# Another start address for the output weights of the second MoE in each half stretch of blocks

## The chip, the cores and the metric

The kernel runs on one core of a Trainium2 chip. Its time is the device time of one execution in microseconds (us), and the number that counts is the median of several executions. Five engines work side by side and meet at semaphores: TensorE (PE, with its weight loads shown apart as PEld), VectorE (DVE), ScalarE (ACT), GpSimd (POOL) and SyncE (SP). DMAs are issued from the queues of SP, ACT and POOL and carried out by 16 DMA engines.

## What is computed

A chunked attention, then two feed-forward blocks ("MoE" in the names), all in float32 from input to output:

```
attention:  out[c] = softmax(q[c] k_full.T / 8) v_full     # 24 chunks of 32 rows, 8 heads, batch 4
first MoE:  xn = x / rms(x) * rms_g                        # 3072 tokens, 512 columns
            y  = (silu(xn @ w_gate) * (xn @ w_val)) @ w_out    # 1536 inner columns
second MoE: h  = y @ w_in                                  # 2048 inner columns
            g  = h if h >= 1, 0 if h <= -1, else (h + 1)^2 / 4
            out = g @ w_out                                # [2048, 512]
```

The change touches the operand of the last line alone: the second `w_out`.

## The kernel before

**Stages.** Six token tiles of 512 tokens go through the kernel. The first four are done one at a time by the plain first MoE, with the attention of later tiles in the gaps. The last two go through the first MoE as a pair, in a form with 7 products in place of 8 (`proj1`, then `out1p`). Then the second MoE takes the six tiles as three pairs: `proj2` makes the inner columns, `out2` multiplies them by `w_out`.

**Precision by three products.** Each float32 operand is kept as a high and a low part (type fp32r), and each product is three matmuls: high times high, high times low, low times high. A matmul has a stationary operand (128 columns, loaded by a weight load) and a moving operand (512 columns, streamed past it).

**`out2`.** It writes tokens on the rows, so the inner columns `hi`, `lo` are stationary and the weights move. For one block b (128 inner columns) and each of 4 token groups m it runs L990 to L992: `hi` against `wh`, `hi` against `wl`, `lo` against `wh`. So a block is 12 matmuls, all of which read one weight tile `wo` of 128 x 2 x 512 (high part, then low part; 4096 bytes in each partition). There are 16 blocks in each of the six calls (3 pairs, and o = 0 or 1 in each pair), 96 blocks in all, 1152 matmuls.

**Order of the work.** In a pair, each `proj2(g)` of g = 0 to 7 is 42 matmuls, and behind it stand two blocks of `out2` with o = 0 (from g = 1 on; in the later pairs, g = 0 is followed by the last two blocks of the pair before). After the eighth come the last two blocks of o = 0 and 14 blocks of o = 1 in a row; the last two of o = 1 wait for the next pair, or end the kernel.

**The weight ring.** `load_wo(i)` takes a tile from a pool with four buffers under the tag `wo` and has SP load it from the DRAM tile `w2o_d` (pieces of 2048 bytes). Blocks 4 to 95 are loaded behind the last matmul of the block four earlier (`load_wo(i + 4)`). The first MoE uses the same function and the same tag for its own 24 loads (i below `2 * F1` = 24), with the weights as stationary operand (L546 to L548). Its call for i = 24 to 27 already draws four tiles of the second MoE from the first MoE's pool `p1`; these are loaded and not read, and the same four blocks are loaded again from the pool `m2` when the second MoE begins. So there are 100 loads from `w2o_d`.

**Queues near the first pair.** SP carries out its DMAs in the order of the program. At the start of the pair of the first MoE it issues four `wo` loads and behind them the loads of `wall` from `w1p_d` (`load_wp`, L763), on which `proj1` runs. POOL's queue at that time still writes converted weights of the second MoE to DRAM (`lo_s`, L200 and L201, from the tile `s12` or `s34`). A tile that is placed where an earlier one lay waits for the last reader of the earlier one, DMAs included.

Of the kernel before, what the change touches and what calls it, by code (L numbers as in the profile page):

```python
# [9 lines left out]
F32R = mybir.dt.float32r  # L10
# [6 lines left out]
P = 128  # L17
# [13 lines left out]

TT = 512
PT = 256
D = 64
FILL = 352

# [2 lines left out]
def tile_stream_attention_moe_moe2(  # L39
# [12 lines left out]
    F1 = wts1.shape[0] // 3  # L52
    F2 = wts2.shape[0] // 2
    KK = DM // P
    NTT = NT // TT
    NU = q.shape[0]
    SCALE = 1.0 / float(D) ** 0.5

    pool = lambda name, bufs, **kw: ctx.enter_context(tc.tile_pool(name=name, bufs=bufs, **kw))
# [245 lines left out]
    m2 = {"single": True, "pace": 0.0}  # L305
# [43 lines left out]
    def load_qk(u):  # L349
# [5 lines left out]
        else:  # L355
            kt = [att.tile([P, TT], F32, tag=f"k{hp}", name="k_in") for hp in range(2)]
            qt = att.tile([P, 2 * PT], F32, tag="q", name="q_in")
        for hp in range(2):
# [4 lines left out]
    def load_v(u):  # L363
        if u >= NU:
            return
        n = 8 * (D + 1)
        if u < 4:
            if not tails:
                tails.append(xs.tile([P, 4, 2, D + 1], F32, tag="xn", name="v_tail"))
            tail = tails[0][:, u]  # L370
            nc.sync.dma_start(tail, v[u].rearrange("p (h c) -> p h c", h=2)[:, :, n - D - 1:])
            vt = [xs.tile([P, TT], F32, tag=f"x{'hl'[hp]}{u}", name="v_in") for hp in range(2)]
            m = n - D - 1
        else:
# [9 lines left out]
    def step_s(u, ps):  # L384
        kt, qt = qk_t.pop(u)
        for hp in range(2):
            for blk in range(2):
                for j in range(4):
                    for par in range(2):
# [4 lines left out]
                            ps[32 * j:32 * j + 32, par, o:o + 64],  # L394
                            qt[p0:p0 + 64, hp * PT + 32 * c:hp * PT + 32 * c + 32],
                            kt[hp][p0:p0 + 64, 64 * c:64 * c + 64],
# [51 lines left out]
    def part_n(u):  # L448
        pr, hh = divmod(u, 2)
        ps = ps_t.pop(("v", u))  # L450
        if hh == 0:
# [8 lines left out]
        nc.vector.tensor_scalar(  # L460
            out=rd.unsqueeze(3), in0=ov[:, :, :, D:D + 1], scalar1=1e-9, scalar2=None, op0=ALU.add
        )
# [144 lines left out]
    for st in ORDER.split():  # L607
        c, n = st[0], st[1:]
# [32 lines left out]
        elif c in "HL":  # L641
            kk, o = divmod(n, 2)
            part = slice(o * PT, o * PT + PT)
            if c == "H":
# [3 lines left out]
        elif c == "G":  # L648
            cols = slice(n % 2 * PT, n % 2 * PT + PT)
            for x in x_t[n // 2]:  # L650
# [101 lines left out]
    wo = {}  # L752
# [12 lines left out]
    def load_wo(i):  # L765

        if i < 2 * F1:
            src = w1o_d[i % F1]
        elif i < 2 * F1 + 2 * NP2 * F2:
            n, u = divmod((i - 2 * F1) % F2, 2)  # L770
            src = w2o_d[n][:, :, u]
        else:
            return
        if i in (0, 2 * F1):
            m2["limit"] = 2 * F1 if i == 0 else 1 << 30
        if i < m2["limit"]:
            wo[i] = m2["pool"].tile([P, 2, 512], F32R, tag="wo", name="wo", bufs=4)
            nc.sync.dma_start(wo[i].bitcast(F32), src)


# [186 lines left out]
    def out1p(o, blocks):  # L967

        last = F1 - 1 in blocks and len(blocks) > 1
        order = [(f, m) for m in range(KK) for f in blocks] if last else [(f, m) for f in blocks for m in range(KK)]  # L970
        for f, m in order:
            sl = slice(m * P, (m + 1) * P)
            w = wo[o * F1 + f]
            mm3(ps_y[m], (w[:, 0, sl], w[:, 1, sl]), hs["1", f, o], f == 0, f == F1 - 1)
            if m == KK - 1:
                load_wo(o * F1 + f + 4)
            if f == F1 - 1:
                evac(m, y_d[NS + o][:, m], nc.sync)

    def out2(pr, o, blocks):  # L980

        M = range(TT // P)
        last = F2 - 1 in blocks
        order = [(b, m) for m in M for b in blocks] if last else [(b, m) for b in blocks for m in M]
        for b, m in order:
            sl = slice(m * P, (m + 1) * P)
            i = 2 * F1 + (2 * pr + o) * F2 + b
            hi, lo = hs[F2 * pr + b, o]
            wh, wl = wo[i][:, 0], wo[i][:, 1]
            nc.tensor.matmul(ps_y[m], hi[:, sl], wh, start=b == 0, stop=False)  # L990
            nc.tensor.matmul(ps_y[m], hi[:, sl], wl, start=False, stop=False)  # L991
            nc.tensor.matmul(ps_y[m], lo[:, sl], wh, start=False, stop=b == F2 - 1)  # L992
            if m == TT // P - 1:
                load_wo(i + 4)
            if b == F2 - 1:
                evac(m, rows(2 * pr + o, m), nc.scalar)
# [17 lines left out]
    for i in range(4):  # L1014
        load_wo(i)
# [45 lines left out]
def _layouts(i):  # L1061
# [4 lines left out]
    M = i["mem_k"].shape[2]  # L1066
    C, NP = S // _CHUNK, S // PT
    W = _CHUNK + _LEFT + _RIGHT + M

    def heads(a):  # L1070

        return a.reshape(B, H // 4, 2, 2, NP, C // NP, *a.shape[3:])
# [20 lines left out]
    q = heads(i["q"].reshape(B, H, C, _CHUNK, D))  # L1093
    q = q.transpose(0, 4, 1, 3, 7, 2, 5, 6).reshape(B * NP * H // 4, 2 * D, 2 * PT)
    kw = heads(kw).transpose(0, 4, 1, 3, 7, 2, 5, 6).reshape(B * NP * H // 4, 2 * D, -1)
# [44 lines left out]
```

## Time and profile before

| | |
|---|---|
| median of 3 runs | 1179.24 us (1176.91 to 1180.4) |
| span of the profiled execution, first to last instruction | 1172.9 us |
| PE busy | 1151.0 us, 98% of the span |
| DVE, ACT, POOL busy | 741.2, 517.6, 108.0 us |
| mean DMA rate | 238 GB/s |
| chain of work that ended last | 86% PE, 6% DMA, 4% DVE |

The span leaves out what lies before the first and after the last instruction: 1179.24 - 1172.9 = 6.3 us against the median. "Busy" counts each matmul from its start to its modelled end; matmuls overlap in the pipeline, so what a matmul costs is the time from its start to the start of the next one, and not its duration.

### The profile page before, as it was taken

The numbers are of one execution on the slowest core, as the hardware profiler recorded it, in microseconds if no ns is written. First come the engines' busy times: TensorE is split into PE (matmuls) and PEld (weight loads), VectorE is DVE, ScalarE is ACT, GpSimd is POOL, SyncE is SP. The second block draws the span as 40 slices with busy tenths as digits, with TensorE's granted clock in tenths as the row PEclk, the third lists the DMA queues.
The fourth block names the chain that finished last, engine by engine and source line by source line (L and its number), as shares of the span: only waits on it lengthen the run. The fifth ranks groups of instructions, "written<-read, shape, count | busy, mean of one in ns | idle before, by whom it ended". The sixth has DMA issues, their size and how long they took to land.

```text
span 1172.9 us, 19949 instructions
## 1 busy us (share of the span) xinstructions
PE 1151.0 (98%) x7993; PEld 936.4 (80%) x7993; DVE 741.2 (63%) x1280; ACT 517.6 (44%) x910; POOL 108.0 (9%) x175
## 2 busy tenths in 40 slices
PE   6899999999999999999999999999999999999998
PEld 4677878887778778878888888888888888888887
DVE  5888865566465655877677576665376662576620
ACT  4766756556665664433333343333143341343310
POOL 2200012212122122201111000000000000000000
PEclk9899999999999999999999999999999999999999
DMA  8566467788767666598898775757466576555364
GB/s 307 177 221 208 153 223 275 282 290 294 276 206 239 223 199 225 199 383 311 305 361 309 283 279 189 261 187 267 158 222 260 195 259 203 191 190 197 135 202 157
DMA packets 98589, 278.60 MB, mean 238 GB/s; under 512 B 10560, under 2 KB 22848, under 8 KB 92096
## 3 DMA queue, kind: packets, MB, share of 16 engines
q1 hardware_dynamic: 79936, 218.59, 52.5%
q0 software_dynamic: 15104, 52.44, 12.3%
q10 hardware_dynamic: 3456, 6.29, 1.4%
q8 instruction: 63, 1.03, 0.3%
q14 instruction: 30, 0.25, 0.1%
HBM read 209.13 MB, written 68.16 MB: 236 GB/s over the span
## 4 chain that ended last, share of the span: by engine, by line
PE 86%; DMA 6%; DVE 4%; ACT 2%; issue 1%; POOL 0%; SPq 0%; ACTq 0%; DVEq 0%; POOLq 0%
PE ps_y L991 7%; PE ps_y L992 7%; PE ps_y L990 7%; PE ps_g L546 6%; PE ps_g L547 6%; PE ps_g L548 6%; PE ps_b L855 5%; PE ps_b L854 5%; PE ps_b L856 5%; PE ps_y L546 5%; PE ps_y L547 5%; PE ps_y L548 5%; PE ps_g L854 4%; PE ps_g L855 4%; PE ps_g L856 4%; DMA w<-in_w_dram 3%
## 5 line engine op out<-in xcount | busy, mean ns | idle before, releaser
L546 PE MATMUL ps_g<-xh,wall 128*128 128x512 f32 x384 | 156.3, 407 | 0.0
L547 PE MATMUL ps_g<-xl,wall 128*128 128x512 f32 x384 | 150.9, 393 | 0.0
L548 PE MATMUL ps_g<-xh,wall 128*128 128x512 f32 x384 | 150.4, 392 | 0.0
L914 ACT ACTIVATE t<-t,half 128x512 f32<-128x512 f32 x96 | 69.0, 720 | 131.2 <-DVE t L913 131.2
L991 PE MATMUL ps_y<-wo,wall 128*128 128x512 f32 x324 | 126.0, 389 | 0.0
L990 PE MATMUL ps_y<-wo,wall 128*128 128x512 f32 x324 | 126.0, 389 | 0.0
L992 PE MATMUL ps_y<-wo,wall 128*128 128x512 f32 x324 | 126.0, 389 | 0.0
L854 PE MATMUL ps_b<-wall 128*128 128x512 f32 x288 | 112.0, 389 | 0.0
L855 PE MATMUL ps_b<-wall 128*128 128x512 f32 x288 | 112.0, 389 | 0.0
L856 PE MATMUL ps_b<-wall 128*128 128x512 f32 x288 | 112.0, 389 | 0.0
L928 DVE TENSOR_TENSOR t<-t,ps_g 128x512 f32<-128x512 f32 x24 | 16.5, 688 | 113.5 <-PE ps_g L856 107.9
L548 PEld LDWEIGHTS ps_g<-xh,wall 128*128 128x128 f32 x384 | 72.6, 189 | 16.1
L854 PE MATMUL ps_g<-wall 128*128 128x512 f32 x216 | 84.2, 390 | 1.1 <-DMA wall<-w1p_d 1.0
L546 PEld LDWEIGHTS ps_g<-xh,wall 128*128 128x128 f32 x384 | 72.6, 189 | 15.8
L855 PE MATMUL ps_g<-wall 128*128 128x512 f32 x216 | 84.1, 389 | 0.0
L856 PE MATMUL ps_g<-wall 128*128 128x512 f32 x216 | 84.0, 389 | 0.0
L547 PEld LDWEIGHTS ps_g<-xl,wall 128*128 128x128 f32 x384 | 72.8, 190 | 13.5
L546 PE MATMUL ps_y<-hh,wall 128*128 128x512 f32 x192 | 77.6, 404 | 0.0
L547 PE MATMUL ps_y<-hl,wall 128*128 128x512 f32 x192 | 75.2, 392 | 0.1
L548 PE MATMUL ps_y<-hh,wall 128*128 128x512 f32 x192 | 74.9, 390 | 0.0
L990 PEld LDWEIGHTS ps_y<-wo,wall 128*128 128x128 f32 x324 | 60.8, 188 | 12.7
L991 PEld LDWEIGHTS ps_y<-wo,wall 128*128 128x128 f32 x324 | 60.8, 188 | 12.6
(157 smaller groups left out, 2240.4 us busy)
## 6 DMA issues: line engine op xcount, KB each, us to landing
wo<-w2o_d SPq DMA_DIRECT2D x100, 512.0 KB, 4.8
wall<-w2p_d SPq DMA_DIRECT2D x24, 1792.0 KB, 7.3
wall<-w1p_d SPq DMA_DIRECT2D x12, 1792.0 KB, 8.6
w<-in_w_dram SPq DMA_DIRECT2D x36, 512.0 KB, 3.9
w<-in_w_dram POOLq DMA_DIRECT2D x32, 512.0 KB, 5.5
k_in<-in_k_dram SPq DMA_DIRECT2D x48, 256.0 KB, 4.6
wo<-w1o_d SPq DMA_DIRECT2D x24, 512.0 KB, 7.9
v_in<-in_v_dram SPq DMA_DIRECT2D x40, 260.0 KB, 4.3
```

Source lines behind the costliest of these rows:

```text
L546: nc.tensor.matmul(ps, wh, xh, start=start, stop=False)
L547: nc.tensor.matmul(ps, wh, xl, start=False, stop=False)
L548: nc.tensor.matmul(ps, wl, xh, start=False, stop=stop)
L854: nc.tensor.matmul(bank, wh, xh, start=st, stop=False, skip_group_check=True)
L855: nc.tensor.matmul(bank, wh, xl, start=False, stop=False, skip_group_check=True)
L856: nc.tensor.matmul(bank, wl, xh, start=False, stop=kk == 1, skip_group_check=True)
L914: nc.scalar.activation(s, s, AF.Square, scale=0.5, bias=half)
L928: tt(out=u2, in0=a, in1=b2, op=ALU.add)
L990: nc.tensor.matmul(ps_y[m], hi[:, sl], wh, start=b == 0, stop=False)
L991: nc.tensor.matmul(ps_y[m], hi[:, sl], wl, start=False, stop=False)
L992: nc.tensor.matmul(ps_y[m], lo[:, sl], wh, start=False, stop=b == F2 - 1)
```

## The change

The tile drawn for a block of the second MoE gets 1152 columns in place of 1024 (4608 bytes in each partition in place of 4096), and the weights lie in it from column `STARTS[k]` on, where k counts half stretches of eight blocks (two to each of the six calls of `out2`). `F2` is 16, so k runs from 0 to 11. The twelve offsets are 8, 16, 24, 48, 4, 56, 64, 96, 128, 192, 256 and 384 bytes.

```diff
+STARTS = (2, 4, 6, 12, 1, 14, 16, 24, 32, 48, 64, 96)
...
         if i < m2["limit"]:
-            wo[i] = m2["pool"].tile([P, 2, 512], F32R, tag="wo", name="wo", bufs=4)
+            if i < 2 * F1:
+                wo[i] = m2["pool"].tile([P, 2, 512], F32R, tag="wo", name="wo", bufs=4)
+            else:
+                k = (i - 2 * F1) // (F2 // 2)
+                w = m2["pool"].tile([P, 1152], F32R, tag="wo", name="wo", bufs=4)
+                wo[i] = w[:, STARTS[k]:STARTS[k] + 1024].rearrange("p (h c) -> p h c", h=2)
             nc.sync.dma_start(wo[i].bitcast(F32), src)
```

No engine gets another instruction or another order. What else moves is addresses. In the built programs every buffer of `wo` in `m2` begins 32 bytes past a multiple of 64, before and after (4608 is 72 times 64), so before the change all 96 blocks are read from such a start, and after it from 40, 48, 56, 16, 36, 24, 32, 0, 32, 32, 32 and 32 bytes past a multiple of 64, for k = 0 to 11. The tiles `h0` to `h4` and `e2` behind the ring move up by 2048 bytes. Since the tag `wo` of pool `p1` also gets the larger size, three of the four buffers of the first MoE's own loads move up by 1536, 1024 and 512 bytes; the one that moves by 1536 now also covers part of the old tile `s34`.

That changes some waits. On SP, at the start of the first MoE's pair, this stood before (names in brackets are the semaphores that the DMA waits for; DMASW are those of DMAs from POOL's queue, DMAHW those from the other queues):

```order
L778 DMA wo<-w1o_d_144 128x1024 [waits PE_49]
L778 DMA wo<-w1o_d_145 128x1024 [waits DMASW7_49,DMASW3_49]
L778 DMA wo<-w1o_d_146 128x1024 [waits DMASW7_49]
L778 DMA wo<-w1o_d_147 128x1024 [waits DMAHW3_49]
L763 DMA wall<-w1p_d_134 128x3584 [waits DMASW2_49,DMAHW4_49,DMASW1_49,DMAHW5_49,DMASW0_49,PE_49]
```

and this stands there now:

```order
L784 DMA wo<-w1o_d_144 128x1024 [waits PE_49]
L784 DMA wo<-w1o_d_145 128x1024 [waits DMASW5_49,DMASW7_49,DMASW3_49,DMASW1_49]
L784 DMA wo<-w1o_d_146 128x1024 [waits DMASW7_49]
L784 DMA wo<-w1o_d_147 128x1024 [waits DMAHW3_49]
L764 DMA wall<-w1p_d_134 128x3584 [waits DMAHW4_49,DMASW2_49,DMAHW5_49,DMASW0_49,PE_49]
```

The second of the four loads has taken over the wait for DMASW1 (the DMA out of `s34`), which before stood at no `wo` load, and one for DMASW5.

## Rows read from the trace of the kernel before

**Rows 1.** The page: busy time by engine, granted clock in 40 slices.

```profile
PE 1151.0 (98%) x7993; PEld 936.4 (80%) x7993; DVE 741.2 (63%) x1280; ACT 517.6 (44%) x910; POOL 108.0 (9%) x175
PEclk9899999999999999999999999999999999999999
```

**Rows 2.** PE's waits: line, releaser, us in total, times, longest.

```profile
PE ps_a L519 <- ACT xn L535: 2.7, 1, 2.7
...
PE ps_g L854 <- DMA wall<-w1p_d: 1.0, 1, 1.0
```

**Rows 3.** Timeline of PE in `out2`: start us, us, what; 12 starts apart.

```profile
1125.42 0.39 PE L991 MATMUL ps_y<-wo,wall 128*128 128x512 f32 x1
...
1128.14 0.39 PE L991 MATMUL ps_y<-wo,wall 128*128 128x512 f32 x1
```

**Rows 4.** Timeline of PE in `proj1`, where `wall` moves; 12 starts apart.

```profile
619.91 0.39 PE L856 MATMUL ps_g<-wall 128*128 128x512 f32 x1
...
622.63 0.39 PE L856 MATMUL ps_b<-wall 128*128 128x512 f32 x1
```

**Rows 5.** Stretches: us, busy (count) by engine, granted clock, DMA share, GB/s.

```profile
8.00:20.00 12.00, 6.68 (x310) 5.05 (x298) 5.80 (x13) 3.62 (x7) 0.00 (x0) 0.97 1.05 375
...
497.00:508.00 11.00, 11.00 (x50) 9.13 (x49) 7.87 (x13) 4.40 (x8) 1.43 (x3) 1.00 1.00 390
508.00:520.00 12.00, 11.09 (x49) 8.83 (x48) 10.55 (x18) 5.39 (x9) 1.24 (x2) 1.00 1.03 425
...
720.00:745.00 25.00, 25.00 (x112) 20.71 (x111) 17.04 (x29) 9.51 (x15) 0.00 (x0) 1.00 0.67 243
...
798.96:820.72 21.76, 21.76 (x97) 18.02 (x96) 13.63 (x12) 7.09 (x7) 0.00 (x0) 1.00 0.71 241
...
1125.39:1147.15 21.76, 21.76 (x97) 18.02 (x96) 0.69 (x1) 0.00 (x0) 0.00 (x0) 1.00 0.72 240
```

**Rows 6.** Timeline of PE: fill matmuls, transposes, attention with 64 and 65 columns.

```profile
8.62 0.77 PE L95 MATMUL ps_s<-busy 128*128 128x352 bf16 x4
...
159.20 0.60 PE L423 MATMUL ps_a<-ident,e 128*128 128x128 f32 x4
162.47 0.86 PE L393 MATMUL ps_a<-k_in,q_in 64*32 64x64 f32 x64
166.25 0.86 PE L439 MATMUL ps_a<-v_in,aT 64*32 64x65 f32 x64
```

**Rows 7.** Lines L423 and L95 on PE: count, duration ns min/median/max, first and last.

```profile
L423 PE MATMUL ps_a<-ident,e x76: 270/272/327, 65.9 to 429.4; 128*128 128x128 f32 x76
...
L95 PE MATMUL ps_s<-busy x16: 312/322/501, 8.6 to 37.5; 128*128 128x352 bf16 x16
```

**Rows 8.** Issues of `wo` in 1128:1150 us: duration, then issue to landing.

```profile
L778 SPq DMA_DIRECT2D wo<-w2o_d x9: 517/517/519, 1128.1 to 1149.9; - x9
...
DMA to landing us min/median/max: 3.3/4.3/5.3
```

**Rows 9.** The page, DMA issues: count, KB each, median us to landing.

```profile
wo<-w2o_d SPq DMA_DIRECT2D x100, 512.0 KB, 4.8
...
v_in<-in_v_dram SPq DMA_DIRECT2D x8, 227.5 KB, 4.8
v_tail<-in_v_dram SPq DMA_DIRECT2D x4, 65.0 KB, 5.2
```

**Rows 10.** Timeline of POOL near 496 us.

```profile
495.50 0.65 POOL L201 DMA_DIRECT2D w2p_d<-s  x1 [1.32 <-DVE s L199]
...
496.69 0.54 POOL L201 DMA_DIRECT2D w2p_d<-s  x1
```

**Rows 11.** Timeline of SP's queue near 500 us.

```profile
499.56 6.09 SPq L778 DMA_DIRECT2D wo<-w1o_d  x4
506.88 0.32 SPq L763 DMA_DIRECT2D wall<-w1p_d  x1
```

**Rows 12.** Line L201 in 494:499 us: time to landing of its two DMAs.

```profile
DMA to landing us min/median/max: 8.4/9.6/10.8
```

**Rows 13.** SP's waits: line, releaser, us in total, times, longest.

```profile
SPq L778 <- DMA w2p_d<-s: 2.1, 1, 2.1
```

**Rows 14.** Timeline of PE where `proj1` first waits for `wall`.

```profile
518.70 0.39 PE L548 MATMUL ps_y<-wall,wo 128*128 128x512 f32 x1
520.06 0.47 PE L854 MATMUL ps_g<-wall 128*128 128x512 f32 x1 [0.97 <-DMA wall<-w1p_d]
```

**Rows 15.** The chain that ended last, that place: start us, us, what.

```profile
506.88 13.04 DMA wall<-w1p_d
```

## The prediction

> **What bounds the kernel now.** I read the page first: PE is busy 98% of the span, and its clock stands at the upper of its two levels (2.4 GHz) in nearly every slice [rows 1]. A busy share of matmuls can hide gaps, so the list of PE's waits comes next: the longest is 2.7 us, and from the first MoE's pair to the end only one wait for a DMA is left, 0.97 us for `wall` [rows 2, 14]. So whatever lengthens a matmul's turn on PE lengthens the kernel by the same amount, and whatever the DMAs or SP do costs nothing until it passes its slack. The changed operand is the moving one of `out2`, so I then took the distance of starts there. In [rows 3] twelve starts take 1128.14 - 1125.42 = 2.72 us, 226.7 ns each, and the window of a half stretch holds 96 turns (and one cut by its edge) in 21.76 us [rows 5]: 96 x 226.7 ns = 21.76 us, nothing idle. The durations of 0.39 us in these rows are longer than a turn, since matmuls overlap. Where `wall` moves in place of `wo`, twelve starts take 622.63 - 619.91 = 2.72 us too [rows 4].
>
> The sum is made on the profiled execution, 1172.9 us of span; 6.3 us lie around it against the median of 1179.24, and I carry them over unchanged. A difference of 0.3% is 3.5 us, about what a measurement can tell from none. Half stretches pass that only together or at a high price: 3.5 us over 96 turns is 37 ns a matmul in one of them, or 3 ns in all twelve.
>
> **The change, part by part.**
>
> *Instructions and order.* None added, none removed, the same order on each engine: 0 us.
>
> *PE's reads of `wo`.* The 1152 matmuls of `out2` read 512 columns (2048 bytes in each partition) from a new start. The trace shows no fp32r matmul from such a start, since every moving tile of that type begins 32 bytes past a multiple of 64. The cost is bounded from both sides. Above: the four transposes of [rows 6] move float32 columns at (0.60 - 0.27)/3 = 109 ns for 128 columns (0.27 is the median duration [rows 7]), so 436 ns for 512: a read that fell to that rate would cost 209 ns a turn, 20.1 us in a half stretch. Below: the four fill matmuls (bf16, 352 columns) take (0.77 - 0.32)/3 = 150 ns a turn (0.32 from [rows 7]), so 218 ns for 512: 8.6 ns less a turn, 0.83 us in a half stretch, 9.9 us in all twelve. I take 0. The nearest rows are the two attention rows of [rows 6]: one reads 64 columns from starts 256 bytes apart, the other 65 columns from starts 260 bytes apart, so three of four of its starts are off a multiple of 16 bytes and half are off a multiple of 8. Both take 0.86 us for 64 instructions. They are plain float32 and so short that their issue may set the pace, which keeps a cost of less than a factor possible; that is why both ends stay in the range.
>
> The Trainium skill, "SBUF — State Buffer" (Door 1, the box on cachelines) says that memory lines are 16 bytes long and that each step to a new line pays a penalty. By it a start off a multiple of 16 (k = 0, 2, 4, 5) touches 129 lines in place of 128; an estimate from that page is under 1% of a turn, some 0.7 us over those four half stretches, and the time by it 1180.4 us in place of 1179.7. The same page says under "Operand start alignment" that any multiple of the element size is legal and that its runs timed nothing; no run here shows more yet.
>
> *Weight loads.* `h0` to `h4` move by 2048 bytes and keep their place within 64 bytes, and so do the first MoE's `wo` tiles (512, 1024, 1536 bytes): 0 us.
>
> *DMAs into `wo`.* Same number, size and pieces. In the 14 blocks in a row each load is issued behind block b for block b + 4, whose turn comes three blocks later: 3 x 2.72 = 8.16 us. Landing takes 3.3 to 5.3 us there [rows 8], so about 2.9 us are free. DMAs are busy 0.71 to 0.72 of that time at 240 GB/s [rows 5], of which `wo` moves 524 kB per 2.72 us = 193 GB/s, so about 0.58 of the share. It takes pieces 1.5 times as long before 0.72 + 0.29 reaches 1 and the ring runs dry. The one transfer in the trace that already lands at starts off 16 bytes is `v_tail` (65 columns a piece): 5.2 us to landing against 4.8 us for its neighbour `v_in` [rows 9]. That is 0.4 us, hidden in 2.9 us: 0 us.
>
> *The new wait on SP.* The second `wo` load of the first MoE's pair now waits until the DMA out of `s34` has landed. POOL issues its two DMAs from L201 at 495.50 and 496.69 us [rows 10]; they take 8.4 and 10.8 us [rows 12], so they land at 503.9 and 507.5. SP today waits 2.1 us for the first of them at the third load [rows 13], and gets to the load of `wall` at 506.88, when PE has freed its buffer [rows 11]. Now SP stands still until about 507.5, and behind it are queued three `wo` loads and that load of `wall`, for which PE waits already. With 0.32 us [rows 11] to 0.9 us for each of the three loads before it, `wall` is issued at about 508.6 to 510.2: 1.7 to 3.3 us later. That would be PE's loss if its 13.04 us to landing [rows 15] were latency. They are mostly queue: DMAs are busy 1.00 of the time from 497 to 520 us, at 390 to 425 GB/s [rows 5], so a later issue delays little as long as transfers that are queued already fill the engines. Ends: 0 and 3.3 us; I take 0.5 us, nearer the lower end by those shares. Loads behind wait for PE and not for SP: no more.
>
> *Waits in the second MoE.* The first use of `h1` to `h3` now names other DMAs, loads into `p1` from the end of the first MoE, while those tiles are first written behind several products; the first load into `m2` loses one wait: 0 us.
>
> Sum: 0 + 0 + 0 + 0 + 0.5 + 0 = +0.5 us: 1172.9 to 1173.4 of span, 1179.7 us of time.
>
> **The rivals.**
>
> *An odd start halves the read (slower).* If PE takes fp32r columns in pairs or lines, a start off that unit could cost a second access for each. It decides from 37 ns a turn in one half stretch. Its price at the rate of the transposes is 20.1 us: with the 4-byte offset alone (k = 4) 1199.8 us, with all four starts off 16 bytes (k = 0, 2, 4, 5) 1179.7 + 80.4 = 1260.1. A smaller toll, 10 ns a turn in the six half stretches that start off 32 bytes, is 5.8 us: 1185.5. Against it stand the two equal attention rows, for it that they may be paced by their issue.
>
> *A better start is faster.* A turn of 226.7 ns is 8.6 ns above the rate of the fill matmuls. If the start 32 bytes past a multiple of 64 were the reason, k = 7 alone would be cured (it starts at a multiple of 64): 0.8 us, not to be told from nothing. Only if most other starts cure it too does it count: all but the five that keep the 32 (k = 6, 8 to 11), so seven half stretches, give 5.8 us: 1173.9. For it: all streams share that start and that rate. Against: nothing but bf16 shows another rate.
>
> The Trainium skill, "TensorE: Matmul & The Clock Gate" (Back-to-back issue gap), gives 216 ns for an isolated turn of 512 columns at the upper clock; this trace shows 226.7, and no run here says yet what the 11 ns are; were all of them due to the start and cured in those seven half stretches, the time by that page would be 1172.3 us.
>
> *DMAs into odd starts are slow (slower).* If pieces landing off a multiple of 32 bytes (k = 0 to 5) took twice as long, the share in the 14 blocks in a row (k = 2 and 3) would go to 0.72 + 0.58 = 1.30, and PE would wait 0.30 x 21.76 = 6.5 us in each: 13 us, 1192.7. Between `proj2` the share is 0.67 at 243 GB/s [rows 5] and `wo` is two loads in 42 + 24 turns (14.96 us, 70 GB/s) there, so 0.19 of it: 0.86, no wait. It decides from 1.5 times. Against it: `v_tail`.
>
> *The wait on SP costs its whole bound.* 3.3 us: 1182.5, which is still within 0.3%; only with a second miss of `wall` behind it is it more.
>
> **How the numbers follow.** No change that counts (1176.2 to 1182.8): 0.74, by the equal rates of all streams and the hidden DMAs. Odd start: 0.13, of which 0.06 small and 0.07 at 1199 and over. Slow DMAs 0.04, more from SP's wait 0.03: slower 0.20. Faster by a better start: 0.06. The range runs from 1176 to 1188, which takes in the forecast with the upper end of SP's wait and the small toll (0.74 + 0.06 + 0.03 = 0.83) and leaves out the gain and the high prices.
>
> **What would show it.** Right: starts in `out2` 226.7 ns apart in all twelve half stretches, windows of 21.76 us, no wait of PE for `wo`; SP's four loads ending near 508 and PE's wait for `wall` near 520 us between 1 and 4 us. Wrong: a half stretch with another distance of starts (the odd start if it is k = 4, or 0, 2, 4, 5; the better start if shorter); or PE waiting for `wo` with a landing over 8 us in k = 2, 3 (slow DMAs).

## The result and the profile after

| | before | after |
|---|---|---|
| median of 4 runs each | 1179.80 us (1176.91 to 1180.4) | 1185.18 us (1184.7 to 1186.66) |
| ratio after / before | | 1.0058 [1.0036, 1.008] |
| span of the profiled execution | 1172.9 us | 1182.9 us |
| PE busy | 1151.0 us | 1156.8 us |

By the ratio of the runs the change made the kernel slower by 0.36 to 0.8%, more than the 0.3% that a measurement can tell from nothing; the two medians alone are 5.4 us apart, 0.46%. The time lies in the predicted range; the case held for the likeliest, no change, did not come. The profiled execution after took 1184.7 us, 1.8 us more than its span. So of the 6.3 us between the span of before and its median, about 1.8 lie around the span, and the rest is that this execution lay below the median (1172.9 + 1.8 = 1174.7 us, less than each of the four runs). The span difference of 10.0 us therefore holds some run-to-run variation, and the ratio is the better measure.

First one line of `out2` from the page of before, then the engines and the lines of `out2` from the page of after (columns of the lines: line, engine, names and shapes, count, busy us, mean ns of one, idle before). L996 to L998 are L990 to L992 of before; L860 of `proj1` is for comparison. The last line is the DMA issue that answers to [rows 9].

```profile
L991 PE MATMUL ps_y<-wo,wall 128*128 128x512 f32 x324 | 126.0, 389 | 0.0
```

```profile
PE 1156.8 (98%) x7993; PEld 936.0 (79%) x7993; DVE 740.2 (63%) x1280; ACT 517.2 (44%) x910; POOL 107.6 (9%) x175
...
L996 PE MATMUL ps_y<-wo,wall 128*128 128x512 f32 x324 | 127.9, 395 | 0.0
L997 PE MATMUL ps_y<-wo,wall 128*128 128x512 f32 x324 | 127.7, 394 | 0.0
L998 PE MATMUL ps_y<-wo,wall 128*128 128x512 f32 x324 | 127.7, 394 | 0.0
L860 PE MATMUL ps_b<-wall 128*128 128x512 f32 x288 | 112.0, 389 | 0.0
...
wo<-w2o_d SPq DMA_DIRECT2D x100, 512.0 KB, 4.6
```

The matmuls of `out2` became longer, 394 to 395 ns against 389 before, and against 389 for `proj1`, with no idle time before them. The loads land as early as before (4.6 against 4.8 us). A mean hides whether all or some are longer, so next comes the distance of twelve starts, the view of [rows 3]: the timeline of PE after, in half stretches k = 2, 4 and 10 (offsets 24, 4 and 256 bytes).

```profile
809.64 0.40 PE L997 MATMUL ps_y<-wo,wall 128*128 128x512 f32 x1
...
812.46 0.40 PE L997 MATMUL ps_y<-wo,wall 128*128 128x512 f32 x1
...
866.35 0.40 PE L996 MATMUL ps_y<-wo,wall 128*128 128x512 f32 x1
...
869.21 0.40 PE L996 MATMUL ps_y<-wo,wall 128*128 128x512 f32 x1
...
1141.70 0.39 PE L996 MATMUL ps_y<-wo,wall 128*128 128x512 f32 x1
...
1144.42 0.39 PE L996 MATMUL ps_y<-wo,wall 128*128 128x512 f32 x1
```

Twelve starts take 2.82, 2.86 and 2.72 us: 235 and 238 ns a turn, and in k = 10 the 226.7 ns of [rows 3]. Whole half stretches say the same. Windows of after for k = 2, 3, 10 and 11 (us, then PE, PEld, DVE, ACT and POOL busy with counts, granted clock, DMA share, GB/s; the last one lacks the final turn):

```profile
803.55:826.04 22.49, 22.49 (x98) 18.14 (x96) 12.65 (x11) 7.09 (x7) 0.00 (x0) 1.00 0.66 221
826.04:848.43 22.39, 22.39 (x98) 18.27 (x97) 2.45 (x4) 0.60 (x1) 0.00 (x0) 1.00 0.50 164
1134.20:1155.98 21.78, 21.78 (x97) 18.02 (x96) 0.69 (x1) 0.00 (x0) 0.00 (x0) 1.00 0.71 233
1155.98:1178.14 22.16, 22.16 (x96) 17.83 (x95) 0.69 (x1) 1.19 (x2) 0.00 (x0) 1.00 0.46 151
```

PE is busy all the time at the full clock in each; 21.76 us of [rows 5] became 22.49 and 22.39, while k = 10 stayed at 21.78. DMA traffic does not order them: the free one has the largest DMA share. Worked out in the same way, turn by turn from the timeline:

| k | 0 | 1 | 2 | 3 | 4 | 5 | 6 | 7 | 8 | 9 | 10 | 11 |
|---|---|---|---|---|---|---|---|---|---|---|---|---|
| offset, bytes | 8 | 16 | 24 | 48 | 4 | 56 | 64 | 96 | 128 | 192 | 256 | 384 |
| ns a turn | 232.7 | 231.6 | 234.3 | 233.2 | 238.0 | 231.3 | 229.0 | 233.6 | 233.0 | 233.3 | 226.9 | 233.3 |

The surplus over 226.7 ns, times 96 turns, summed over the twelve, is 6.7 us. From the first matmul of `out2` to the end the two profiles differ by 7.6 us (482.4 against 474.8). Of the other 0.9 us, 0.5 lie in the first ten turns of `proj2` behind each group of `out2` blocks, which begin at 231 to 232 ns and come back to 227, and 0.4 behind the start of the last matmul (4.8 against 4.4 us; e1 below, which pays no toll, has 4.8 there too).

The second place is SP's queue, which answers to [rows 11, 13 to 15]. Timeline of after, SP's queue and then PE where `proj1` first waits for `wall`:

```profile
500.71 8.93 SPq L784 DMA_DIRECT2D wo<-w1o_d  x4
509.80 0.32 SPq L764 DMA_DIRECT2D wall<-w1p_d  x1
...
521.38 0.47 PE L860 MATMUL ps_g<-wall 128*128 128x512 f32 x1 [1.14 <-DMA wall<-w1p_d]
```

The line of SP's waits after (us in total, times, longest):

```profile
SPq L784 <- DMA w2p_d<-s: 6.0, 1, 6.0
```

The chain that ended last, after, at that place (start us, us, what):

```profile
497.83 10.27 DMA w2p_d<-s
...
509.80 11.44 DMA wall<-w1p_d
```

SP stood still for 6.0 us in place of 2.1, until the DMA out of `s34` landed (497.83 + 10.27 = 508.10). The load of `wall` was issued 509.80 - 500.71 = 9.09 us after the first of the four loads, where it was 506.88 - 499.56 = 7.32 before: 1.8 us later. It took 11.44 in place of 13.04 us to land, and PE waited 1.14 in place of 0.97 us.

### The profile page after: what moved, and what is told of

Its sections match the earlier page's. It is cut to its first block, busy times and chain, and to the rows that moved or that the text cites. A ratio compares the mean times of both kernels' runs of the same rounds, so it can differ in the third digit from the quotient of the medians.

```text
span 1182.9 us, 19946 instructions
## 1 busy us (share of the span) xinstructions
PE 1156.8 (98%) x7993; PEld 936.0 (79%) x7993; DVE 740.2 (63%) x1280; ACT 517.2 (44%) x910; POOL 107.6 (9%) x175
## 4 chain that ended last, share of the span: by engine, by line
PE 85%; DMA 5%; DVE 5%; ACT 2%; issue 2%; SPq 1%; POOL 0%; ACTq 0%; DVEq 0%; POOLq 0%
PE ps_y L996 8%; PE ps_y L998 8%; PE ps_y L997 8%; PE ps_g L547 6%; PE ps_g L549 6%; PE ps_g L548 6%; PE ps_b L861 5%; PE ps_b L860 5%; PE ps_b L862 5%; PE ps_y L547 4%; PE ps_y L548 4%; PE ps_y L549 4%; PE ps_g L860 4%; PE ps_g L861 4%; PE ps_g L862 4%
## 5 line engine op out<-in xcount | busy, mean ns | idle before, releaser
L996 PE MATMUL ps_y<-wo,wall 128*128 128x512 f32 x324 | 127.9, 395 | 0.0
L997 PE MATMUL ps_y<-wo,wall 128*128 128x512 f32 x324 | 127.7, 394 | 0.0
L998 PE MATMUL ps_y<-wo,wall 128*128 128x512 f32 x324 | 127.7, 394 | 0.0
L860 PE MATMUL ps_b<-wall 128*128 128x512 f32 x288 | 112.0, 389 | 0.0
L860 PE MATMUL ps_g<-wall 128*128 128x512 f32 x216 | 84.4, 391 | 1.2 <-DMA wall<-w1p_d 1.1
L998 PEld LDWEIGHTS ps_y<-wo,wall 128*128 128x128 f32 x324 | 61.1, 189 | 14.5
```

Of the source, the lines that this page charges most:

```text
L860: nc.tensor.matmul(bank, wh, xh, start=st, stop=False, skip_group_check=True)
```

## The experiments

Three theories of the longer turns stood against each other: that a matmul pays by the distance between the start of its moving and the start of its stationary operand (1), that it pays by the start of the moving operand alone (2), and that the slack, the loads or a moved neighbour did it (3). In each kernel the distance of starts was read as above. Each ratio is to runs of the kernel before that were taken with the experiment: their median is 1175.98 us for e1, e2, e3 and e6, 1176.27 for e8, e9 and e10, and one run of 1176.34 stands beside e4, e5 and e7.

**e1_slack: the larger buffers, all twelve offsets zero.**

```diff
-STARTS = (2, 4, 6, 12, 1, 14, 16, 24, 32, 48, 64, 96)
+STARTS = (0,) * 12
```

> All of the change but the offsets: buffers of 4608 bytes, every STARTS 0. Theories: (1) distance - a matmul of out2 pays by the distance between the start of its moving and of its stationary operand, modulo 256 bytes; (2) start - it pays by the start of its moving operand alone, modulo 256 bytes; (3) surroundings - the time comes from the slack, the moved tiles, the waits and the landings, not from where PE reads. (1) and (2): 226.7 ns a turn in all of out2 (21.76 us in each half stretch), the time within 2.5 us of before; the wait on SP stays, with PE's wait for wall at 1.0 to 1.3 us. (3): as after, 5 us over before.

Turns are 226.7 ns everywhere, as (1) and (2) had it; the time is 1180.7 us, 1.0042 [1.0027, 1.0057] of before. These 4.7 us lie outside the 2.5 us of (1) and (2) and near the 5 us of (3), so no theory had both. A line of e1's page, then two of PE's waits in e1, then PE's timeline at the pair:

```profile
L996 PE MATMUL ps_y<-wo,wall 128*128 128x512 f32 x324 | 126.1, 389 | 0.0
```

```profile
PE ps_g L860 <- DMA wall<-w1p_d: 2.6, 1, 2.6
...
PE ps_y L547 <- DMA wo<-w1o_d: 1.3, 2, 1.1
```

```profile
524.62 0.47 PE L860 MATMUL ps_g<-wall 128*128 128x512 f32 x1 [2.56 <-DMA wall<-w1p_d]
...
526.45 0.63 PE L861 MATMUL ps_g<-wall 128*128 128x512 f32 x1
526.88 0.63 PE L862 MATMUL ps_g<-wall 128*128 128x512 f32 x1
```

The slack makes no turn longer, so the toll in `out2` belongs to the offsets. What the slack does cost stands at the pair: the wait for `wall` is 1.6 us longer than in [rows 14], and behind it seven turns take 526.88 - 526.45 = 0.43 us in place of 0.227, and the one before them 0.39, which adds 1.6 us. In the window from 519 to 531 us the granted clock is 0.86; turns of 427 ns for 512 columns are the lower of its two levels, 1.2 GHz. That makes 3.2 us. The 1.3 us of waits for `wo` stand at 661 and 665 us, far behind the pair's start, and e5 and e8, which lack the larger buffers in `p1`, have such waits too (1.7 and 1.0 us), so they are not shown to come from the slack. This profile is of the slowest of e1's four runs (1183.19 us); what the rest of the 4.7 us is was not shown.

**e2_all4 and e3_all256: one offset for all, 4 or 256 bytes.**

```diff
-STARTS = (2, 4, 6, 12, 1, 14, 16, 24, 32, 48, 64, 96)
+STARTS = (1,) * 12        # e2_all4
+STARTS = (64,) * 12       # e3_all256
```

> Every block of the second MoE lies 4 bytes into its buffer. (1) and (2): about 238 ns a turn in all 1152 matmuls, as in the half stretch that had this offset, so 1152 x 11.3 ns = 13.0 us over the kernel with all offsets 0. (3): as that kernel.

> Every block lies 256 bytes into its buffer. (1) and (2), with a period of 256 bytes: 226.7 ns a turn everywhere, the time of the kernel with all offsets 0 within 2 us. (3): the same as with any offset. If it pays, the half stretch with 256 bytes was free for another reason than its offset.

Measured: 1192.1 us, 1.0139 [1.0122, 1.0156], with turns of 238.1 ns in all twelve half stretches; and 1178.24 us, 1.0017 [1.0005, 1.0029], with 226.7 ns in all twelve. The difference is 13.9 us (e2 to e1: 11.4); 1152 turns of 11.4 ns more are 13.1 us. So the toll is a fixed price a turn that adds up in full, and it belongs to the offset and not to the stage or half stretch. Between e1 and e3, whose turns are the same, the medians differ by 2.5 us, a little over the 2 us that the expectation allowed: so much is not told by the turns. A line from the page of e2, the same from that of e3, and PE's timeline of e3 at the pair:

```profile
L997 PE MATMUL ps_y<-wo,wall 128*128 128x512 f32 x324 | 130.0, 401 | 0.0
```

```profile
L997 PE MATMUL ps_y<-wo,wall 128*128 128x512 f32 x324 | 126.1, 389 | 0.0
```

```profile
522.06 0.47 PE L860 MATMUL ps_g<-wall 128*128 128x512 f32 x1 [2.55 <-DMA wall<-w1p_d]
```

The last shows the same long wait for `wall` as in e1, but in e3 the turns behind it stayed at 0.23 us. So the fall of the clock does not follow every wait of that length.

**e6_sweep: twelve other offsets.**

```diff
-STARTS = (2, 4, 6, 12, 1, 14, 16, 24, 32, 48, 64, 96)
+STARTS = (8, 20, 28, 36, 40, 44, 52, 56, 60, 63, 80, 128)
```

> Twelve further offsets, one in each half stretch: 32, 80, 112, 144, 160, 176, 208, 224, 240, 252, 320 and 512 bytes. (1) and (2): 512 bytes free (226.7 ns a turn), 320 bytes like 64 (229 ns), the others between 227 and 238 ns, so 1 to 9 us in all. A turn below 226.7 ns at any of them would make an offset that is worth having; neither theory forbids it, and I expect none. (3): no pattern by offset.

A single run, 1184.06 us. Together with the kernels above the toll, in ns a turn above 226.7, is this:

| offset, bytes | 0 | 4 | 8 | 16 | 24 | 32 | 48 | 56 | 64 | 80 | 96 | 112 | 128 |
|---|---|---|---|---|---|---|---|---|---|---|---|---|---|
| toll, ns | 0 | 11.3 | 6.0 | 4.9 | 7.6 | 6.8 | 6.5 | 4.6 | 2.3 | 4.5 | 6.9 | 0 | 6.3 |

| offset, bytes | 144 | 160 | 176 | 192 | 208 | 224 | 240 | 252 | 256 | 320 | 384 | 512 |
|---|---|---|---|---|---|---|---|---|---|---|---|---|
| toll, ns | 6.6 | 7.3 | 4.3 | 6.6 | 7.8 | 6.6 | 6.6 | 4.4 | 0 | 2.4 | 6.6 | 0 |

No alignment of the start orders this: 96, 128 and 192 pay, 112 does not. It repeats after 256 bytes (64 and 320, 128 and 384; 0, 256 and 512), and none is below 0. (One turn of 310 ns in the half stretch with 208 is left out.) Two starts of e6 at 112 bytes, twelve apart:

```profile
807.80 0.39 PE L996 MATMUL ps_y<-wo,wall 128*128 128x512 f32 x1
...
810.52 0.39 PE L996 MATMUL ps_y<-wo,wall 128*128 128x512 f32 x1
```

2.72 us: free. What lies at a fixed place, so that an offset of 112 could be as good as none? The stationary operand does. In the trace it bears the name of the buffer in which `hi` and `lo` lie: `wall` for 81 blocks, `h` for 15. In the program of before, both start at the same place modulo 256 bytes as `wo`, so the table's offset is also the distance from the stationary start to the moving start, which is theory (1). The next three kernels tell (1) from (2).

**e4_both_moved and e5_h_moved: the kernel before, with a small tile ahead of others.**

```diff
+    m2["pool"].tile([P, 48], F32, name="gap")    # e4: ahead of the wo ring: wo and h move by 192 bytes
+    m2["pool"].tile([P, 16], F32, name="gap")    # e5: behind the ring: h alone moves by 64 bytes
```

> The kernel before, with 192 bytes put ahead of the wo buffers of the second MoE, so that wo and the tiles h0 to h4 behind it both start 192 bytes further and wall stays. 972 matmuls of out2 have their stationary operand in wall, 180 in h. (1) distance: 233.3 ns a turn with wall (the distance is now 192, as in the half stretch with 192 bytes), 226.7 with h (distance 0). (2) start: 233.3 with both. (3): 226.7 with both.

> The kernel before, with 64 bytes put ahead of h0 to h4 alone; wo and wall stay. (1) distance: the 180 matmuls with h stationary have a distance of -64, which is 192 modulo 256: 233.3 ns a turn (229 if only the size of the distance counts and not its sign); with wall 226.7. (2) start: 226.7 with both, since no moving operand moved.

A single run each, 1181.0 and 1177.29 us beside 1176.34 of before. The groups of PE in e4 and then in e5:

```profile
L992 PE MATMUL ps_y<-wo,wall 128*128 128x512 f32 x324 | 127.7, 394 | 0.0
L990 PE MATMUL ps_y<-wo,h 128*128 128x512 f32 x60 | 23.4, 390 | 0.0
```

```profile
L990 PE MATMUL ps_y<-wo,wall 128*128 128x512 f32 x324 | 126.2, 389 | 0.0
L990 PE MATMUL ps_y<-wo,h 128*128 128x512 f32 x60 | 23.7, 396 | 0.0
```

In e4 the same tile `wo`, moved by 192 bytes, costs 233.3 ns a turn against `wall`, which did not move, and against `h`, which moved with it, 226.7 once some seven turns behind each change of the stationary tile are past (227.8 over all 180). In e5 `wo` lies where it always lay, and the turns against the moved `h` take 233.3 ns. So the start of `wo` does not set the price by itself; the distance does. e5 also gives the sign: `h` up by 64 is a distance of -64, or 192 modulo 256, and 233.3 is the price of 192 in the table and not that of 64 (229.0).

**e7_first_moe: the other way round, in another stage.** In the first MoE's pair `wo` is stationary and `wall` moves. Here `wo` gets tiles of 1040 columns with the data from column 16, so that its four buffers lie 64, 128, 192 and 256 bytes off their old places (the blocks take them in the order 64, 256, 192, 128), while `wall` stays.

```diff
-            wo[i] = m2["pool"].tile([P, 2, 512], F32R, tag="wo", name="wo", bufs=4)
+            if i < 2 * F1:
+                w = m2["pool"].tile([P, 1040], F32R, tag="wo", name="wo", bufs=4)
+                wo[i] = w[:, 16:1040].rearrange("p (h c) -> p h c", h=2)
+            else:
+                wo[i] = m2["pool"].tile([P, 2, 512], F32R, tag="wo", name="wo", bufs=4)
```

> The kernel before, with the output weights of the first MoE (stationary there, with wall moving) in buffers of 4160 bytes, 64 bytes into each; the second MoE as before in time of use but in those four first buffers. In turn the distance of moving from stationary start is 192, 0, 64 and 128 bytes modulo 256 in the first MoE's pair (288 matmuls, twelve a block). (1) distance: 233, 226.7, 229 and about 233 ns a turn, repeating every four blocks; out2 226.7. (2) start: 226.7 everywhere, since wall did not move.

A single run, 1180.98 us. Blocks in the four buffers, one after the other, twelve starts each, on PE's timeline:

```profile
569.64 0.40 PE L546 MATMUL ps_y<-wall,wo 128*128 128x512 f32 x1
...
572.44 0.39 PE L858 MATMUL ps_g<-wall 128*128 128x512 f32 x1
...
581.99 0.39 PE L546 MATMUL ps_y<-wall,wo 128*128 128x512 f32 x1
...
584.71 0.39 PE L858 MATMUL ps_g<-wall 128*128 128x512 f32 x1
...
594.23 0.39 PE L546 MATMUL ps_y<-wall,wo 128*128 128x512 f32 x1
...
596.98 0.39 PE L858 MATMUL ps_g<-wall 128*128 128x512 f32 x1
```

2.80, 2.72 and 2.75 us, then 2.80 again (from 606.50 to 609.30): 233.4, 226.7, 229 and 233 ns. By the table, distances of 192, 0, 64 and 128 cost 233.3, 226.7, 229.0 and 233.0. The rule holds in another stage, for the stationary operand moved in place of the moving one.

**e8_toll_alone and e9_wait_alone: the two costs apart.** e8 is the kernel after, but pool `p1` keeps tiles of 4096 bytes. e9 is the kernel before, but `p1` alone gets 1152 columns, with the data at the start.

```diff
-            if i < 2 * F1:
+            if i < 2 * F1 or "m2" not in m2:        # e8
...
+    m2["m2"] = True                                 # once the pool m2 is made
```

```diff
-            wo[i] = m2["pool"].tile([P, 2, 512], F32R, tag="wo", name="wo", bufs=4)
+            if "m2" in m2:                          # e9
                 wo[i] = m2["pool"].tile([P, 2, 512], F32R, tag="wo", name="wo", bufs=4)
+            else:
+                w = m2["pool"].tile([P, 1152], F32R, tag="wo", name="wo", bufs=4)
+                wo[i] = w[:, :1024].rearrange("p (h c) -> p h c", h=2)
...
+    m2["m2"] = True                                 # once the pool m2 is made
```

> The change with its twelve offsets in the second MoE, but the first MoE's pool keeps its buffers of 4096 bytes, so that SP's waits ahead of the load of wall stand as before the change. If the change costs two things, the distance between the two starts in out2 and the new wait on SP, this keeps the first alone: half stretches as in the changed kernel, 6.5 to 7.5 us of toll in out2, the load of wall issued 9.7 us after the first matmul of the first MoE's pair, PE's wait for it 0.9 to 1.2 us. If the toll were the only cost, the time would equal that of the changed kernel.

> The kernel before with the first MoE's pool alone in buffers of 4608 bytes (offset 0), the second MoE untouched: the new wait on SP alone. Out2 226.7 ns a turn. The load of wall issued 11.5 to 13 us after the start of the pair, PE's wait for it 1.3 to 2.7 us in place of 1.0, so 0.3 to 1.7 us over before; up to 2 us more in executions in which TensorE's clock falls after that wait, as in the kernel with all offsets 0. If the wait were free (the load only queues later), the time would be that of before within 0.5 us.

e8: 1183.45 us, 1.0054 [1.0038, 1.007], 4.5 to 8.2 us. e9: 1177.66 us, 1.0017 [0.9999, 1.0034], -0.1 to 4.0 us. One line of PE's waits and one of SP's from e8, the line of PE's from e9, and e9's timeline of SP's queue and of PE:

```profile
PE ps_g L860 <- DMA wall<-w1p_d: 0.9, 1, 0.9
...
SPq L784 <- DMA w2p_d<-s: 2.9, 1, 2.9
```

```profile
PE ps_g L858 <- DMA wall<-w1p_d: 3.3, 1, 3.3
```

```profile
499.69 9.81 SPq L782 DMA_DIRECT2D wo<-w1o_d  x4
...
522.57 0.47 PE L858 MATMUL ps_g<-wall 128*128 128x512 f32 x1 [3.34 <-DMA wall<-w1p_d]
...
524.00 0.63 PE L859 MATMUL ps_g<-wall 128*128 128x512 f32 x1
524.42 0.63 PE L860 MATMUL ps_g<-wall 128*128 128x512 f32 x1
```

Without moved buffers in `p1`, SP waits 2.9 us for the DMA out of POOL's queue, near the 2.1 of before and not the 6.0 of after, PE's wait for `wall` is 0.9 us, and nearly the whole loss remains: it is the toll. With the moved buffers alone the wait is there, 3.3 us in this profile (1.3 to 2.7 were expected), with the lower clock behind it for seven turns of 427 ns, as in e1. That profile is of one of e9's slower runs (1180.99 us).

**e10_wall_first: can the wait for `wall` that before already has be had back?** Loads 1 to 3 of the pair are moved behind the load of `wall`.

```diff
-    for i in range(4):
-        load_wo(i)
+    load_wo(0)
...
+        if f == 0:
+            for i in range(1, 4):
+                load_wo(i)
```

> The kernel before, with three of the four wo loads at the start of the first MoE's pair moved behind the load of wall for which PE waits. If that load lands late because of what SP has queued ahead of it (wait and 1.5 MB of wo), PE's wait of 1.0 us for it goes and the time falls by about 1 us; if it lands late because the DMA engines are full whatever the order, the wait stays near 1.0 us.

1175.55 us, 0.9996 [0.9975, 1.0016]: no difference. The timeline of SP's queue in e10, then a line of PE's waits and its place on PE's timeline:

```profile
499.85 1.24 SPq L778 DMA_DIRECT2D wo<-w1o_d  x1
507.22 0.32 SPq L763 DMA_DIRECT2D wall<-w1p_d  x1
507.64 1.56 SPq L778 DMA_DIRECT2D wo<-w1o_d  x3
```

```profile
PE ps_y L546 <- DMA wo<-w1o_d: 1.8, 1, 1.8
```

```profile
655.21 0.50 PE L546 MATMUL ps_y<-wall,wo 128*128 128x512 f32 x1 [1.79 <-DMA wo<-w1o_d]
```

`wall` is issued no earlier (PE frees its buffer only then), but with fewer transfers ahead of it lands after 8.7 us in place of 13.0, and PE's wait for it is gone. The three loads moved behind it cost PE nothing: from 500 to 650 us its list holds no wait for a load. The 1.8 us for `wo` stand at 655 us, at the end of the pair, where e1, e5, e8 and e9 wait 1.0 to 1.7 us for such loads as well. So the 1.0 us is had back at its place, and whether the kernel gains it is not shown: the interval, 2.9 us less to 1.9 us more, is wider than the gain.

## Why the prediction was right or wrong

**PE's reads of `wo`: the step that failed.** "I take 0", and "nearest rows are the two attention rows". It was 0 to 11.3 ns a turn, 6.7 us in sum, inside the wide bounds but not at the value taken; half stretches with another distance of starts are what the prediction itself had named as the sign of being wrong. That the time still lay within the range is luck: the range was drawn to take in a small toll of another cause. Two things went wrong. First, the attention rows could not show it: they are plain float32 with 64 and 65 columns, and the prediction itself said that their issue may set the pace. A toll of 5% on a long fp32r stream is not to be seen there, so equal rows were no reason for 0. Secondly, the quantity was the wrong one. The prediction read that "every moving tile of that type begins 32 bytes past a multiple of 64" and asked what other starts of the moving operand cost. What mattered is where the stationary tile begins: in `out2` of before it begins at the same place modulo 256 as the moving one, and the change left that place in eleven of twelve half stretches. e4, e5 and e7 show this. In the built program of before the same holds for all 4680 fp32r matmuls of 512 columns, `proj1` of [rows 4] among them: their two operands begin at the same place modulo 256, so no row of that trace could show the toll, and equal rates there spoke neither for nor against it.

**"An odd start halves the read": wrong as a mechanism, near by its size.** Its small form, 10 ns in the six half stretches off 32 bytes, gave 1185.5 us and 1185.18 was measured. But multiples of 32 pay as well (k = 7, 8, 9 and 11), k = 6 pays 2.3 ns, and only k = 10 is free. Its large form, 209 ns a turn, did not come at all: k = 4 pays 11.3. That this number fits is chance.

The Trainium skill's box on cachelines ("SBUF — State Buffer", Door 1), from which the prediction worked out 0.7 us for the four starts off 16 bytes, does not order these tolls: offsets that are multiples of 16 (48, 96, 128, 192) pay 6.5, 6.9, 6.3 and 6.6 ns, and those off it (4, 8, 24, 56) 11.3, 6.0, 7.6 and 4.6. The same page of the Trainium skill, under "Who interferes with whom", says that PE never waits on anyone, and the Trainium skill, "TensorE: Matmul & The Clock Gate", under "Step-by-step: what each phase is for", that loading the next weights takes no read bandwidth from the running matmul. Read for this case, these leave no room for a toll at any distance; measured are 226.7 to 238.1 ns a turn, depending on where the two operands of a matmul lie to each other. That it is the weight load that disturbs the stream is not shown.

**"A better start is faster": none found.** Of 25 offsets, 21 distances modulo 256, none goes below 226.7 ns. What the 11 ns are between this and the 216 ns that the Trainium skill, "TensorE: Matmul & The Clock Gate" (Back-to-back issue gap), gives, no run here shows.

**The new wait on SP: right in its working, small in its price.** "`wall` is issued at about 508.6 to 510.2": it was 509.80, and counted from the first of the four loads 1.8 us later than before, where 1.7 to 3.3 were forecast. (Three loads of 0.32 us behind 507.5 end at 508.5 and not 508.6, which changes nothing.) The price was to be 0.5 us between 0 and 3.3; it was 0.17 us in the profile of after, and the later issue was indeed made good by a shorter landing. But over five other kernels with the same moved buffers PE's wait was 1.7 to 3.3 us (e1, e2, e3, e6, e9), and in e1 and e9 some 1.6 us more went to the lower clock. That part was not in the sum: the bound counted the wait and not what PE does after it. e9 puts the whole at 0.17%, with 0 just inside its interval; e3 has 0.17% and e1 0.42% with the same buffers and no toll, so this price is known to no better than some us.

**DMAs into `wo`: right.** 4.6 us to landing against 4.8, and 3.5 to 4.1 us for the eight loads issued between 822 and 842 us, in the 14 blocks in a row:

```profile
DMA to landing us min/median/max: 3.5/4.0/4.1
```

No wait of PE for `wo` stands in `out2`, at any offset. **Weight loads, instructions and the second MoE's waits** were to cost 0: e1, with every address moved but no distance changed, has turns of 226.7 ns and no new wait there. The moves were multiples of 256 bytes, which is what counted; the prediction had looked at 64.

**The chances.** The forecast gave 0.74 to no change. It had worked out itself that 3 ns a turn in all twelve half stretches would be seen; with that beside an upper bound of 209 ns, rows that could not show a toll of some ns were too little for such a chance.

**What stays open.** Why the distance matters is not shown. Weight loads run beside the streams most of the time (PEld is busy 79% of the span), so that the two reads get into each other's way is a guess that fits; but why the period is 256 bytes, why 112 bytes is free, and why 4 and 252 differ (11.3 and 4.4 ns), it does not explain. Nor is it shown whether a matmul pays by its own stationary operand or by that of the next matmul, whose weights load meanwhile: within a half stretch of `out2` and within a block of e7 both begin at the same place modulo 256. And no kernel here has fewer weight loads than matmuls, other types or fewer columns at such distances.

## What to carry to other kernels

Where PE is the bound and fp32r matmuls of 512 columns have a weight load each, as here, lay out the tiles so that the moving and the stationary start have the same place modulo 256 bytes; a pad or a small tile in a pool that shifts one and not the other costs 1 to 5% of each turn at most distances (besides 0, only 112 was free), at no instruction and no wait; it shows in the distance of starts, and in a mean duration of 394 in place of 389 ns. A few larger tiles drawn under a tag enlarge every buffer of that tag in the pool and so move its neighbours, so look for the waits that come with it. And an effect for which the trace has no row of the same type and length is not 0 because a distant row is flat.

## What the runs showed of the hardware

- The turn of an fp32r matmul of 512 columns with its own weight load is 226.7 ns at distances of 0, 112, 256 and 512 bytes between the moving and the stationary start, and up to 238.1 ns at others, with a period of 256 bytes.
- A change of distance does not show at once: in the kernel after, the first six turns of k = 10 took 1135.58 - 1134.20 = 1.38 us, 230 ns each, between the 233 of k = 9 and the 226.7 that followed; in e4 some seven turns lay between the two.
- After waits of PE of 2.6 and 3.3 us (e1, e9) the clock fell to 1.2 GHz for seven turns of 427 ns; after one of 2.55 us in the same place (e3) it did not.
